# A Fourier filter ahead of a gated FFN: the transform in steps of four columns instead of two

## The chip, the cores and the metric

The kernel runs on one core of one Trainium2 chip. The metric is the device time of one execution in microseconds, the median of several runs. The engines are TensorE (PE in the profile, its weight loads PEld), VectorE (DVE), ScalarE (ACT), GpSimd (POOL) and SyncE (SP), which here only issues DMA transfers; a core has 16 DMA engines.

## What is computed

A filter is applied to a sequence of 3136 rows in the frequency domain, for 8 batches and 256 channels, and the result goes through an FFN with a gate that is a convolution over three rows.

```python
def _attn_ref(x, filt_r, filt_i):          # x: 8 x 3136 x 256
    X = np.fft.rfft(x, axis=1)
    Y = X * (filt_r + 1j * filt_i)[None]
    return np.fft.irfft(Y, n=x.shape[1], axis=1).astype(np.float32)

def _moe_ref(x, w_in, conv_w, w_out):      # 256 -> 1024 -> 256, kernel of 3
    h = np.maximum(x @ w_in, 0.0)
    conv_out = ...                         # sum over k of conv_w[k] * h shifted by k - 1
    gate = 1.0 / (1.0 + np.exp(-conv_out))
    return (h * gate @ w_out).astype(np.float32)
```

The weights of the FFN come as 64-bit numbers, which the kernel converts itself.

## The kernel before

The length is split as 3136 = 112 x 28, and the transform is four matrix products with steps through DRAM between them.

- **First** (L317 to L322): for one of the 28 columns, 112 rows of x by a 112 x 112 matrix in `s1_sb`. A step does two columns in one PSUM bank (`ps`); `store` (L307) copies them to `sa` on ACT and sends them to `a_dram`.
- **Second** (L324 to L332): for two of the 28 frequency groups `a` is loaded from `a_dram` and multiplied by `s2_sb` (for the last group `s2s_sb`) into `pp`. It needs all 28 columns of its batch in `a_dram`.
- **The filter** (`filt`, L334 to L345): three products on DVE read `pp`: L340 writes `u`, by the real parts in `t1_sb`; L341 and L342 write the two halves of `v`, by the imaginary parts in `t2_sb`. Real and imaginary rows lie on partitions 0 to 55 and 64 to 119, and L341 and L342 cross over. POOL adds `u` and `v` to `z` (L344). `u` has two buffers (the pool's default), `z` three, and `v` is one of two fixed tiles in turn.
- **Third** (L347 to L352): `z` by `i1_sb`, copied to `sb` on ACT and sent to `b_dram`.
- **Last** (`last_load`, `last_stage`, `last_out`): two columns are loaded from `b_dram` into `br`, multiplied by `m2_sb`, and split into a high part (`hi_act` on ACT) and a low part (`lo_dve` on DVE, L149) of `y`, which the FFN reads. Batch 0 is done at the end of the transform, the other batches between the FFN's steps.

The loop at L369 runs over steps `i` of two columns or groups, 14 to a batch. Step `i` does the first transform of step `i - 1`, and with `m = i - 18` the second of `m - 1`, the filter of `m - 2` and the third of `m - 4`. Four engines keep the order in which the code is written; SP's transfers stand in an order close to it. On TensorE a step is third, first, second. x is loaded seven steps ahead (8 buffers), a three steps ahead (5). At the beginning the tables arrive piece by piece: parts of the filter (`load_filter`, L246) go to partitions 0 to 63 of `t1_sb` and `t2_sb`, and ACT copies them to partitions 64 to 119, the imaginary ones with a factor of -1 (L251 to L254). From step 22 on, `convert_weights` makes fp32 of the weights in short DVE instructions (L160 to L172), a POOL sum (L174) and copies, at most one piece in a step. From step 118 on the last transform of batch 0 goes along with the rest, two columns in a step.

Behind the loop the FFN runs over pieces of 448 rows and 128 of its 1024 inner channels (L502 to L522); each product there is three matmuls of high and low parts. PSUM's eight banks are five for `ps` and three for `pp` in the transform, and are given to the FFN's pools after it.

## Time and profile before

| | |
|---|---|
| median of 3 runs | 1573.16 us (1568.74 to 1574.19) |
| the profiled execution | 1572.45 us |
| its span, first to last instruction | 1570.7 us |
| TensorE busy | 1505.0 us (96%), 9424 matmul instructions |
| DVE, ACT, POOL busy | 1280.6, 1189.3, 697.4 us |
| moved by DMA | 166.83 MB |

Times in the profile count from the span's start. A group of instructions is named by its line, engine, operation and tiles (out<-in); its idle time is that of the engine just before such instructions, with the releasers that ended most of it. A matmul of fp32 stands there as two instructions, so "x4" is the two matmuls of a step. Ends of matmuls are modelled, so that starts of matmuls are the better clock.

### The profile page before, as it was taken

The page shows a single profiled execution, that of the slowest core. Times are in us where ns is not written, and L with a number is a line of the kernel's source. Part 1 is how long each engine was busy: PE and PEld are TensorE (multiplying, and loading weights), DVE is VectorE, ACT ScalarE, POOL GpSimd, SP SyncE. Part 2 cuts the span into 40 slices and gives each one's busy share as a digit, 9 for nine tenths or more (in the row PEclk, how much of TensorE's full clock was granted, in tenths as well). Part 3 has the DMA queues.
Part 4 walks back from the last instruction along what each step waited for, and adds up shares of the span by engine and source line. Part 5 has one row for each costly group of instructions (what it writes and reads, how often), then busy time and mean ns, then how long its engine had stood idle before and what let it go on. Part 6 is the DMA issues. An engine that isn't in the chain of part 4 may idle for free.

```text
span 1570.7 us, 26429 instructions
## 1 busy us (share of the span) xinstructions
PE 1505.0 (96%) x9424; PEld 1346.7 (86%) x9424; DVE 1280.6 (82%) x1965; ACT 1189.3 (76%) x2162; POOL 697.4 (44%) x624
## 2 busy tenths in 40 slices
PE   5699999988999999999999999999999999999998
PEld 3356666656999999999999999999999999999998
DVE  0478888888888888888888888888888888888887
ACT  3444444435888888888888888888888888888887
POOL 0255555553444444444444444444444434444444
PEclk9799999999999999999999999999999999999999
DMA  9999999984111011111101111111111111100001
GB/s 285 288 321 337 342 342 346 328 283 140 30 48 48 30 48 48 48 48 48 47 25 36 48 53 48 47 45 47 36 42 48 48 43 36 48 25 24 24 25 48
DMA packets 128278, 166.83 MB, mean 106 GB/s; under 512 B 10682, under 2 KB 87571, under 8 KB 128147
## 3 DMA queue, kind: packets, MB, share of 16 engines
q1 hardware_dynamic: 128147, 165.14, 33.0%
q8 instruction: 75, 1.23, 0.3%
q14 instruction: 56, 0.46, 0.1%
HBM read 88.03 MB, written 77.07 MB: 105 GB/s over the span
## 4 chain that ended last, share of the span: by engine, by line
PE 83%; DMA 10%; DVE 3%; issue 1%; ACT 1%; SPq 1%; POOL 1%; ACTq 0%; DVEq 0%; POOLq 0%
PE ps_h L178 12%; PE ps_h L179 12%; PE ps_h L177 11%; PE po L473 11%; PE po L475 11%; PE po L474 11%; PE ps_h L216 6%; DMA a<-a_dram 4%; PE pp L328 3%; PE ps L351 3%; PE ps L321 2%; DMA a_dram<-sa 2%; DMA t_sb<-in_fi 1%; DVE y L149 1%; DVE v L341 1%
## 5 line engine op out<-in xcount | busy, mean ns | idle before, releaser
L152 POOL TENSOR_TENSOR g<-t,g 128x448 fp32r<-128x448 f32 x448 | 517.2, 1154 | 666.9 <-ACT g L146 262.8
L473 PE MATMUL po<-wo,g 128*128 128x256 f32 x1568 | 441.6, 282 | 0.0
L475 PE MATMUL po<-wo,g 128*128 128x256 f32 x1568 | 433.9, 277 | 0.0
L474 PE MATMUL po<-wo,g 128*128 128x256 f32 x1568 | 433.6, 277 | 0.0
L447 DVE SCALAR_TENSOR_TENSOR t<-ps_h,cw,t 128x448 f32<-128x448 f32 x448 | 305.5, 682 | 83.2 <-ACT t L442 72.9
L178 PE MATMUL ps_h<-y,wi 128*128 128x450 f32 x896 | 330.4, 369 | 4.5 <-DVE y L149 4.5
L177 PE MATMUL ps_h<-y,wi 128*128 128x450 f32 x896 | 328.8, 367 | 3.0 <-ACT y L146 1.6
L179 PE MATMUL ps_h<-y,wi 128*128 128x450 f32 x896 | 328.8, 367 | 0.0
L448 DVE SCALAR_TENSOR_TENSOR t<-ps_h,cw,t 128x448 f32<-128x448 f32 x448 | 306.4, 684 | 16.0
L442 ACT ACTIVATE t<-ps_h,cw 128x448 f32<-128x448 f32 x448 | 284.8, 636 | 42.6 <-ACT ps_h L440 1.9
L473 PEld LDWEIGHTS po<-wo,g 128*128 128x128 f32 x1568 | 294.8, 188 | 7.0
L474 PEld LDWEIGHTS po<-wo,g 128*128 128x128 f32 x1568 | 294.4, 188 | 5.7
L475 PEld LDWEIGHTS po<-wo,g 128*128 128x128 f32 x1568 | 294.5, 188 | 0.0
L440 ACT ACTIVATE ps_h<-ps_h 128x450 f32<-128x450 f32 x448 | 252.0, 562 | 31.6 <-PE ps_h L179 26.8
L453 DVE TENSOR_TENSOR t<-ps_h,t 128x448 f32<-128x448 f32 x448 | 275.1, 614 | 0.1
L452 ACT ACTIVATE t<-t 128x448 f32<-128x448 f32 x448 | 255.0, 569 | 12.2 <-DVE t L448 11.2
L146 ACT ACTIVATE g<-t 128x448 fp32r<-128x448 f32 x448 | 254.6, 568 | 0.2 <-DVE t L453 0.2
L344 POOL TENSOR_TENSOR z<-u,v 120x512 f32<-120x512 f32 x112 | 157.0, 1402 | 181.4 <-DVE v L342 164.8
L309 ACT ACTIVATE sb<-ps 112x512 f32<-112x512 f32 x112 | 66.9, 597 | 161.5 <-DMA b_dram<-sb 86.7
L179 PEld LDWEIGHTS ps_h<-y,wi 128*128 128x128 f32 x896 | 168.3, 188 | 13.9
L177 PEld LDWEIGHTS ps_h<-y,wi 128*128 128x128 f32 x896 | 170.1, 190 | 11.6 <-ACT y L146 2.8
L178 PEld LDWEIGHTS ps_h<-y,wi 128*128 128x128 f32 x896 | 168.3, 188 | 13.5 <-DVE y L149 6.7
(51 smaller groups left out, 1475.0 us busy)
## 6 DMA issues: line engine op xcount, KB each, us to landing
x<-in_x SPq DMA_DIRECT2D x112, 224.0 KB, 4.9
a_dram<-sa SPq DMA_DIRECT2D x112, 224.0 KB, 4.6
a<-a_dram SPq DMA_DIRECT2D x112, 224.0 KB, 4.6
b_dram<-sb SPq DMA_DIRECT2D x112, 224.0 KB, 4.4
br<-b_dram SPq DMA_DIRECT2D x112, 224.0 KB, 2.6
out<-ot SPq DMA_DIRECT2D x27, 896.0 KB, 4.1
raw<-in_w_in SPq DMA_DIRECT2D x8, 256.0 KB, 5.2
raw<-in_w_out SPq DMA_DIRECT2D x8, 256.0 KB, 6.1
```

Source lines behind the costliest of these rows:

```text
L152: nc.gpsimd.tensor_tensor(out=dst, in0=src, in1=hi.bitcast(F32), op=ALU.subtract)
L177: nc.tensor.matmul(ps, lhsT=wh, rhs=rh, start=start, stop=False, **kw)
L178: nc.tensor.matmul(ps, lhsT=wh, rhs=rl, start=False, stop=False, **kw)
L179: nc.tensor.matmul(ps, lhsT=wl, rhs=rh, start=False, stop=stop, **kw)
L442: nc.scalar.activation(t, h[:, 1:SUB + 1], AF.Copy, scale=cw[:, 1, f:f + 1])
L447: nc.vector.scalar_tensor_tensor(out=t, in0=h[:, 0:SUB], scalar=cw[:, 0, f:f + 1], in1=t, op0=ALU.mult, op1=ALU.add)
L448: nc.vector.scalar_tensor_tensor(out=t, in0=h[:, 2:SUB + 2], scalar=cw[:, 2, f:f + 1], in1=t, op0=ALU.mult, op1=ALU.add)
L452: nc.scalar.activation(t, t, AF.Sigmoid)
L453: nc.vector.tensor_mul(t, h[:, 1:SUB + 1], t)
L473: nc.tensor.matmul(o, lhsT=gh[:, sl], rhs=wo[0][:, f], start=first, stop=False, skip_group_check=True)
L474: nc.tensor.matmul(o, lhsT=gh[:, sl], rhs=wo[1][:, f], start=False, stop=False, skip_group_check=True)
L475: nc.tensor.matmul(o, lhsT=gl[:, sl], rhs=wo[0][:, f], start=False, stop=last, skip_group_check=True)
```

## The change

A step does four columns or four groups, and there are 7 steps to a batch instead of 14. Loads and stores of x, sa, a and sb are twice as large and half as many. PSUM tiles of the transform take two banks, two for first and third (`bank_pair`) and two for `pp`, eight banks as before. The buffers are x 4, a 3, sa and sb 2, z 2 and u 1, each of double size. In a step TensorE's order is first, third, second; the third transform is that of `m - 2`, with `m = i - 9`. Loads of a stand one step ahead. Table pieces come at steps 4 to 10. The imaginary parts of the filter are loaded to partitions 56 to 119 and copied down to 0 to 55 without a sign; L349 of the new kernel multiplies by -1 as well. Conversion of the weights takes up to two pieces in a step, from step 11 on, with one buffer for `ws` instead of two. The last transform of batch 0 takes four columns in a step. The FFN's code is the same.

```diff
-        return np.concatenate([re, gap, im, -im, gap, re], 1)
+        return np.concatenate([re, gap, im], 1)
...
-    def last_load(b, c):
-        br = lp.tile([112, 2, D], F32, name="br", bufs=4)
-        nc.sync.dma_start(out=br, in_=b_dram[b][c:c + 2].rearrange("n p d -> p n d"))
+    def last_load(b, c, n=2):
+        br = lp.tile([112, n, D], F32, name=f"br{n}", bufs=4 if n == 2 else 2)
+        nc.sync.dma_start(out=br, in_=b_dram[b][c:c + n].rearrange("n p d -> p n d"))
         lasts[b, c] = br
...
-    def last_stage(b, c, ps):
+    def last_stage(b, c, ps, n=2):

         br = lasts[b, c]
-        for j in range(2):
+        if n == 2:
+            pv = ps[:, 0:4 * N1].rearrange("p (k c a) -> p k c a", c=2, a=N1)
+        else:
+            pv = ps.rearrange("p (k e) -> p k e", k=KT)[:, :, 0:n * N1].rearrange("p k (c a) -> p k c a", a=N1)
+        for j in range(n):
             for k in range(KT):
-                o = ps[:, (2 * k + j) * N1:(2 * k + j + 1) * N1]
-                nc.tensor.matmul(o, lhsT=br[:, j, 128 * k:128 * k + 128], rhs=m2_sb, start=True, stop=True)
-        lasts[b, c] = ps
-
-    def last_out(b, c):
-        yh, yl = y_slices(b, slice(c, c + 2))
-        pv = lasts.pop((b, c))[:, 0:4 * N1].rearrange("p (k c a) -> p k c a", c=2, a=N1)
+                nc.tensor.matmul(pv[:, k, j], lhsT=br[:, j, 128 * k:128 * k + 128], rhs=m2_sb, start=True, stop=True)
+        lasts[b, c] = pv
+
+    def last_out(b, c, n=2):
+        yh, yl = y_slices(b, slice(c, c + n))
+        pv = lasts.pop((b, c))
         hi_act(yh, pv)
         lo_dve(yl, pv, yh)
...
+    NQ = 7
+    SKEW = 9
...
         tc.tile_pool(name="fp", bufs=2) as fp,
-        tc.tile_pool(name="cv", bufs=2) as cv,
-        tc.tile_pool(name="fps", bufs=5, space=bass.MemoryType.PSUM) as fps,
+        tc.tile_pool(name="fps", bufs=2, space=bass.MemoryType.PSUM) as fps,
     ):
...
-        turned = [fc.tile([120, 2, D], F32, name=f"v{k}") for k in range(2)]
+        turned = [fc.tile([120, 4, D], F32, name=f"v{k}") for k in range(2)]
...
-        def load_filter(c):
+        parts = {}
+        psums = {}
+        raws = {}
+
+        def load_tables(c):
+
             sl = slice(4 * c, 4 * c + 4)
-            for t, src in ((t1_sb, fr), (t2_sb, fi)):
-                nc.sync.dma_start(out=t[0:64, sl], in_=src[:, sl])
+            nc.sync.dma_start(out=t1_sb[0:64, sl], in_=fr[:, sl])
+            nc.sync.dma_start(out=t2_sb[56:120, sl], in_=fi[:, sl])
+            nc.sync.dma_start(out=i1_sb[:, sl], in_=i1[:, sl])

         def copy_filter(c):
             sl = slice(4 * c, 4 * c + 4)
             nc.scalar.activation(t1_sb[64:120, sl], t1_sb[0:56, sl], AF.Copy)
-            nc.scalar.activation(t2_sb[64:120, sl], t2_sb[0:56, sl], AF.Copy, scale=-1.0)
+            nc.scalar.activation(t2_sb[0:56, sl], t2_sb[64:120, sl], AF.Copy)
...
-                ws = cv.tile([128, 2, 256], F32, name="ws")
+                ws = cv.tile([128, 2, 256], F32, name="ws", bufs=1)
...
-                    yield
+                yield
...
+        def load(kind, b, q):
             if kind == "x":
+                r = xp.tile([112, 4, D], F32, name="x", bufs=4)
...
+                r = fp.tile([112, 4, D], F32, name="a", bufs=3)
...
+
+        def store(kind, b, q, ps):
+            st = (xp if kind == "sa" else fp).tile([112, 4, D], F32, name=kind, bufs=2)
...
+        def bank_pair():
+            return fps.tile([128, 1024], F32, name="ps")
+
+        def first(b, q):
+            r = rows.pop(("x", b, q))
+            ps = bank_pair()[0:112].rearrange("p (n d) -> p n d", d=D)
+            for j in range(4):
+                nc.tensor.matmul(ps[:, j], lhsT=s1_sb[:, 4 * q + j], rhs=r[:, j], start=True, stop=True)
             return ps
...
-        def filt(b, p):
-
-
-            pp, v = psums.pop((b, p)), turned[p % 2]
-            sl = slice(2 * p, 2 * p + 2)
-            u = fp.tile([120, 2, D], F32, name="u")
+        def second(b, q):
+            r = rows.pop(("a", b, q))
+            pp = fps.tile([120, 4, D], F32, name="pp")
+            for j in (0, 2):
+                if j == 0 or q < NQ - 1:
+                    nc.tensor.matmul(pp[:, j:j + 2], lhsT=s2_sb, rhs=r[:, j:j + 2], start=True, stop=True)
+                else:
+                    nc.tensor.matmul(pp[:, 2], lhsT=s2_sb, rhs=r[:, 2], start=True, stop=True)
+                    nc.tensor.matmul(pp[:, 3], lhsT=s2s_sb, rhs=r[:, 3], start=True, stop=True)
+            psums[b, q] = pp
+
+        def filt(b, q):
+
+
+            pp, v = psums.pop((b, q)), turned[q % 2]
+            sl = slice(4 * q, 4 * q + 4)
+            u = fp.tile([120, 4, D], F32, name="u", bufs=1)
             nc.vector.tensor_mul(u, pp, t1_sb[:, sl])
             nc.vector.tensor_mul(v[64:120], pp[0:56], t2_sb[0:56, sl])
-            nc.vector.tensor_mul(v[0:56], pp[64:120], t2_sb[64:120, sl])
-            z = fp.tile([120, 2, D], F32, name="z", bufs=3)
+            nc.vector.scalar_tensor_tensor(out=v[0:56], in0=pp[64:120], scalar=-1.0, in1=t2_sb[64:120, sl], op0=ALU.mult, op1=ALU.mult)
+            z = fp.tile([120, 4, D], F32, name="z")
             nc.gpsimd.tensor_tensor(out=z, in0=u, in1=v, op=ALU.add)
-            parts["z", b, p] = z
-
-        def third(b, p):
-            z = parts.pop(("z", b, p))
-            ps = fps.tile([112, 2, D], F32, name="ps")
-            for j in range(2):
-                nc.tensor.matmul(ps[:, j], lhsT=i1_sb[:, 2 * p + j], rhs=z[:, j], start=True, stop=True)
+            parts[b, q] = z
...
-        SKEW = NP + 4
...
-        done = NP * B + 6
-        NI = max(NP * B + SKEW + 5, done + N2 // 2 + 3)
+        done = NQ * B + 2
+        NI = NQ * B + SKEW + 5
         with tc.manual_schedule(engines=COMPUTE):
...
                 if i == done:
+                    for _ in wsteps:
+                        pass
...
-                if 1 <= i < 4:
-                    nc.sync.dma_start(out=s1_sb[:, 4 * i + 12:4 * i + 16], in_=s1[:, 4 * i + 12:4 * i + 16])
-                if (bp := at(f + 7)) and i:
+                if i < 3:
+                    nc.sync.dma_start(out=s1_sb[:, 4 * i + 16:4 * i + 20], in_=s1[:, 4 * i + 16:4 * i + 20])
+                if (bp := at(i + 3)) and i:
                     load("x", *bp)
-                if bp := at(m + 3):
+                if bp := at(m + 1):
                     load("a", *bp)
-                if i == 6:
-                    nc.sync.dma_start(out=s2_sb, in_=s2[:, 0:120])
-                    nc.sync.dma_start(out=s2s_sb, in_=s2s[:, 0:120])
+                if i == 3:
+                    nc.sync.dma_start(out=s2_sb, in_=s2)
+                    nc.sync.dma_start(out=s2s_sb, in_=s2s)
                     nc.sync.dma_start(out=m2_sb, in_=m2)
-                if 12 <= i < 26 and i % 2 == 0:
-                    sl = slice((i - 12) // 2 * 4, (i - 12) // 2 * 4 + 4)
-                    load_filter(i // 2 - 6)
-                    nc.sync.dma_start(out=i1_sb[:, sl], in_=i1[:, sl])
-                if bp := at(m - 2):
+                if 4 <= i < 11:
+                    load_tables(i - 4)
+                if bp := at(m - 1):
                     filt(*bp)
-                pt = third(*bp) if (bp := at(m - 4)) else None
-                pf = first(*bp) if (bp := at(f - 1)) else None
-                if bp := at(m - 1):
+                pf = first(*bp) if (bp := at(i)) else None
+                if pf is not None:
+                    store("sa", *at(i), pf)
+                pt = third(*bp) if (bp := at(m - 2)) else None
+                if pt is not None:
+                    store("sb", *at(m - 2), pt)
+                if bp := at(m):
                     second(*bp)
-                if pt is not None:
-                    store("sb", *at(m - 4), pt)
-                if pf is not None:
-                    store("sa", *at(f - 1), pf)
-                if 3 <= i < 16:
-                    next(csteps, None)
-                if i == 16:
+                for _ in range(2):
+                    if 1 <= i < 8:
+                        next(csteps, None)
+                    if i >= 11:
+                        next(wsteps, None)
+                if i == 8:
                     load_weights(0)
                     load_weights(1)
-                if i >= 22 and i % 9 != 8:
-                    next(wsteps, None)
-                if 16 <= i < 30 and i % 2 == 0:
-                    copy_filter(i // 2 - 8)
-                c = 2 * (i - done)
+                if 7 <= i < 14:
+                    copy_filter(i - 7)
+                c = 4 * (i - done - 2)
+                if 0 <= c - 8 < N2:
+                    last_out(0, c - 8, 4)
                 if 0 <= c - 4 < N2:
-                    last_out(0, c - 4)
-                if 0 <= c - 2 < N2:
-                    last_stage(0, c - 2, fps.tile([128, 512], F32, name="ps"))
+                    last_stage(0, c - 4, bank_pair(), 4)
                 if 0 <= c < N2:
-                    last_load(0, c)
+                    last_load(0, c, 4)
...
+    fi = np.roll(fi, 8, 0)
```

On DVE, the first filter steps: `pp` is the second transform in PSUM, `t_sb` a part of the filter, `raw` and `em` are the weights' conversion; in brackets the semaphores that an instruction waits for (Pool is POOL's, PE TensorE's, DMAHW a transfer's). Before:

```order
L340 TENSOR_TENSOR u<-pp,t_sb 120x512 [waits DMAHW2_49,PE_49,Activation_49]
L341 TENSOR_TENSOR v_103<-pp,t_sb 56x512 [waits DMAHW3_49]
L342 TENSOR_TENSOR v_103<-pp,t_sb 56x512 [waits Activation_49,Pool_49]
L340 TENSOR_TENSOR u<-pp,t_sb 120x512 [waits PE_49]
L341 TENSOR_TENSOR v_104<-pp,t_sb 56x512
L342 TENSOR_TENSOR v_104<-pp,t_sb 56x512 [waits Pool_49]
L340 TENSOR_TENSOR u<-pp,t_sb 120x512 [waits PE_49,DMAHW1_49,Activation_49,Pool_49]
```

And after the change, at the same place:

```order
L347 TENSOR_TENSOR u<-pp,t_sb 120x1024 [waits DMAHW7_49,PE_49,Activation_49]
L348 TENSOR_TENSOR v_103<-pp,t_sb 56x1024 [waits Activation_49]
L349 SCALAR_TENSOR_TENSOR v_103<-pp,t_sb 56x1024 [waits DMAHW0_49,Pool_49]
L347 TENSOR_TENSOR u<-pp,t_sb 120x1024 [waits PE_49,DMAHW4_49,Activation_49,Pool_49]
L348 TENSOR_TENSOR v_104<-pp,t_sb 56x1024 [waits Activation_49]
L349 SCALAR_TENSOR_TENSOR v_104<-pp,t_sb 56x1024 [waits DMAHW5_49]
L160 TENSOR_SCALAR em<-raw 128x512 [waits DMAHW1_49,DMAHW0_49]
L162 TENSOR_SCALAR em<-raw 128x512
L347 TENSOR_TENSOR u<-pp,t_sb 120x1024 [waits PE_49,Activation_49,Pool_49]
```

The product into `u` waits for POOL from the third step on before and from the second on after, and two conversions stand together behind L349.

On SP, the transfers around the first load of a (`a_dram_57` is batch 0's, `a_dram_58` batch 1's; `in_fr`, `in_fi` and `in_i` are a piece of the tables). Before:

```order
L304 DMA x<-in_x 112x512
L249 DMA t_sb<-in_fr 64x1024
L249 DMA t_sb<-in_fi 64x1024
L388 DMA i_sb<-in_i 120x448
L315 DMA a_dram_57<-sa 112x2x256
L304 DMA x<-in_x 112x512
L315 DMA a_dram_58<-sa 112x2x256
L304 DMA x<-in_x 112x512
L304 DMA a<-a_dram_57 112x512 x2
```

And after:

```order
L318 DMA a_dram_57<-sa 112x4x256
L307 DMA x<-in_x 112x1024
L258 DMA t_sb<-in_fr 64x1024
L259 DMA t_sb<-in_fi 64x1024
L260 DMA i_sb<-in_i 120x448
L318 DMA a_dram_58<-sa 112x4x256
L307 DMA x<-in_x 112x1024
L307 DMA a<-a_dram_57 112x1024
L258 DMA t_sb<-in_fr 64x1024
```

Another piece of the tables has moved in between the last store of batch 0 and the first load that reads it; four of the seven pieces now stand ahead of that load, two before.

On DVE, the end of the transform (`y` and `ps` are the last transform of batch 0, L447 and L450 the first instructions of the FFN). Before:

```order
L149 TENSOR_TENSOR y_2840<-ps,y_2839 128x2x2x112
L340 TENSOR_TENSOR u<-pp,t_sb 120x512
L341 TENSOR_TENSOR v_104<-pp,t_sb 56x512
L342 TENSOR_TENSOR v_104<-pp,t_sb 56x512
L149 TENSOR_TENSOR y_2840<-ps,y_2839 128x2x2x112 x3
L447 SCALAR_TENSOR_TENSOR t<-ps_h,cw,t 128x448
```

And after:

```order
L149 TENSOR_TENSOR y_1899<-ps,y_1898 128x2x4x112
L347 TENSOR_TENSOR u<-pp,t_sb 120x1024
L348 TENSOR_TENSOR v_103<-pp,t_sb 56x1024
L349 SCALAR_TENSOR_TENSOR v_103<-pp,t_sb 56x1024
L149 TENSOR_TENSOR y_1899<-ps,y_1898 128x2x4x112 x4
L450 SCALAR_TENSOR_TENSOR t<-ps_h,cw,t 128x448
```

Of the subtractions for `y` now four of four columns stand behind the last filter step, where three of two columns stood.

More of the change, by code (lines that the diff above doesn't have):

```diff
@@ L230, in tile_fft_filter_gated_ffn @@
         tc.tile_pool(name="fp", bufs=2) as fp,
-        tc.tile_pool(name="cv", bufs=2) as cv,
-        tc.tile_pool(name="fps", bufs=5, space=bass.MemoryType.PSUM) as fps,
+        tc.tile_pool(name="fps", bufs=2, space=bass.MemoryType.PSUM) as fps,
     ):
+        cv = forward_pools.enter_context(tc.tile_pool(name="cv", bufs=2))
         s2_sb = fc.tile([112, 120], F32, name="s2_sb")
@@ L315, in store @@
             nc.sync.dma_start(out=v, in_=st)
-        def first(b, p):
-            r = rows.pop(("x", b, p))
-            ps = fps.tile([112, 2, D], F32, name="ps")
-            for j in range(2):
-                nc.tensor.matmul(ps[:, j], lhsT=s1_sb[:, 2 * p + j], rhs=r[:, j], start=True, stop=True)
-            return ps
-        def second(b, p):
-            r = rows.pop(("a", b, p))
-            pp = fps.tile([120, 2, D], F32, name="pp", bufs=3)
-            if p < NP - 1:
-                nc.tensor.matmul(pp, lhsT=s2_sb, rhs=r, start=True, stop=True)
-            else:
-                for j, m in ((0, s2_sb), (1, s2s_sb)):
-                    nc.tensor.matmul(pp[:, j], lhsT=m, rhs=r[:, j], start=True, stop=True)
-            psums[b, p] = pp
@@ L344, in filt, with third @@
             nc.gpsimd.tensor_tensor(out=z, in0=u, in1=v, op=ALU.add)
-            parts["z", b, p] = z
-        def third(b, p):
-            z = parts.pop(("z", b, p))
-            ps = fps.tile([112, 2, D], F32, name="ps")
-            for j in range(2):
-                nc.tensor.matmul(ps[:, j], lhsT=i1_sb[:, 2 * p + j], rhs=z[:, j], start=True, stop=True)
+            parts[b, q] = z
+        def third(b, q):
+            z = parts.pop((b, q))
+            ps = bank_pair()[0:112].rearrange("p (n d) -> p n d", d=D)
+            for j in range(4):
+                nc.tensor.matmul(ps[:, j], lhsT=i1_sb[:, 4 * q + j], rhs=z[:, j], start=True, stop=True)
@@ L352, in third @@
             return ps
         def at(i):
-            return divmod(i, NP) if 0 <= i < NP * B else None
-        SKEW = NP + 4
-        nc.sync.dma_start(out=s1_sb[:, 0:4], in_=s1[:, 0:4])
-        load("x", 0, 0)
-        load("x", 0, 1)
-        for c in range(1, 4):
+            return divmod(i, NQ) if 0 <= i < NQ * B else None
+        for c in range(4):
             nc.sync.dma_start(out=s1_sb[:, 4 * c:4 * c + 4], in_=s1[:, 4 * c:4 * c + 4])
-            load("x", 0, 2 * c)
-            load("x", 0, 2 * c + 1)
+            load("x", 0, c)
```

18 lines of the change are left out of this document (4 added, 14 removed).

## The prediction

> **What bounds the kernel now.** I read the slices of the page first: the DMA engines are full for some 340 us and nearly idle after. Then the engines by stretch, cut where that changes: one row for each (start:end, length, busy us and instructions of PE, PEld, DVE, ACT, POOL, then granted clock, DMA share, GB/s):
>
> ```profile
> 0.00:46.00 46.00, 25.15 (x79) 15.85 (x80) 1.18 (x8) 16.83 (x25) 1.51 (x8) 0.86 0.97 283
> 46.00:91.00 45.00, 33.90 (x101) 20.23 (x100) 26.52 (x40) 21.21 (x30) 15.72 (x11) 0.84 1.04 302
> 91.00:321.00 230.00, 216.08 (x831) 145.20 (x830) 192.16 (x289) 100.82 (x178) 131.95 (x103) 1.00 1.00 336
> ...
> 384.00:1571.00 1187.00, 1177.37 (x8175) 1129.56 (x8173) 1004.55 (x1552) 1023.71 (x1892) 518.13 (x476) 1.00 0.13 41
> ```
>
> The last stretch, the gated FFN, is 1187 us of full TensorE, and its code is not touched. So the question is only when it begins. The transform before it has a filling part, a steady part (91 to 321) and a tail. TensorE in the steady part, in order of time (start, length, what):
>
> ```profile
> 92.32 1.03 PE L321 MATMUL ps<-x,s_sb 112*112 112x256 f32 x4
> ...
> 94.91 1.03 PE L321 MATMUL ps<-x,s_sb 112*112 112x256 f32 x4
> ...
> 320.53 1.03 PE L321 MATMUL ps<-x,s_sb 112*112 112x256 f32 x4
> ```
>
> From one first transform to the next is 2.59 us when nothing is waited for (94.91 - 92.32), a third of it, 0.86, for each of the three transforms. From 92.32 to 320.53 there are 81 steps: 2.82 us each, 5.63 for two. TensorE at 2.59 and a DMA share of 1.00 are almost in balance. The waits of that stretch (in all, times, longest):
>
> ```profile
> PE pp L328 <- DMA a<-a_dram: 12.1, 14, 1.9
> ...
> DVE u L340 <- POOL z L344: 1.1, 1, 1.1
> ```
>
> TensorE waits for loads of a. DVE almost never waits for POOL (once): `u` has two buffers, so the products of one step run while POOL still adds those of the last.
>
> **The change, part by part. The loop through u.** `u` is doubled in size and has one buffer. L347 writes it first, L348 and L349 follow on DVE, and POOL's sum (L351 of the new kernel) reads it; so the next L347 waits until the sum of the step before has ended. DVE's three products and POOL's sum, which ran beside each other, now run one after the other. The prices, groups by line and shape (busy, mean ns of one, idle before):
>
> ```profile
> L344 POOL TENSOR_TENSOR z<-u,v 120x512 f32<-120x512 f32 x112 | 157.0, 1402 | 181.4 <-DVE v L342 164.8 <-PE pp L328 10.6 <-PE ps L351 4.7
> L342 DVE TENSOR_TENSOR v<-pp,t_sb 56x512 f32<-56x512 f32 x112 | 77.6, 693 | 3.3
> L340 DVE TENSOR_TENSOR u<-pp,t_sb 120x512 f32<-120x512 f32 x112 | 77.3, 690 | 75.7 <-PE pp L328 67.0 <-POOL z L344 2.3 <-ACT t_sb L254 2.3
> L341 DVE TENSOR_TENSOR v<-pp,t_sb 56x512 f32<-56x512 f32 x112 | 76.6, 684 | 2.9
> L149 DVE TENSOR_TENSOR y<-ps,y 128x448 fp32r<-128x448 f32 x13 | 13.1, 1010 | 2.9 <-ACT y L146 2.4
> L174 POOL TENSOR_TENSOR ws<-ws,em 128x512 f32<-128x512 f32 x8 | 10.2, 1269 | 0.0
> L253 ACT ACTIVATE t_sb<-t_sb 56x1024 f32<-56x1024 f32 x7 | 7.4, 1055 | 0.2
> L164 DVE TENSOR_TENSOR em<-em 128x512 int32<-128x512 int32 x8 | 5.5, 693 | 0.2
> L168 DVE SCALAR_TENSOR_TENSOR ws<-em 128x512 f32<-128x512 int32 x8 | 5.5, 693 | 0.2
> L174 POOL TENSOR_TENSOR cw<-cw,em 128x24 f32<-128x24 f32 x1 | 0.2, 233 | 18.5 <-DVE em L172 18.5
> L164 DVE TENSOR_TENSOR em<-em 128x24 int32<-128x24 int32 x1 | 0.2, 184 | 0.0
> ```
>
> L164 at 512 and at 24 elements gives DVE (693 - 184)/488 = 1.043 ns an element, so 512 more cost 0.534 us and the products become 1.224, 1.218 and 1.227: 3.67 us. L174 gives POOL (1269 - 233)/488 = 2.12 ns, so 512 more cost 1.09 us. What stands between them, and what holds a sum back, in order of time:
>
> ```profile
> 319.90 0.69 DVE L164 TENSOR_TENSOR em<-em 128x512 int32<-128x512 int32 x1
> 320.63 0.69 DVE L340 TENSOR_TENSOR u<-pp,t_sb 120x512 f32<-120x512 f32 x1
> 322.75 0.43 DVE L166 TENSOR_SCALAR em<-raw 128x512 int32<-128x512 int32 x1
> ...
> 332.92 0.69 DVE L342 TENSOR_TENSOR v<-pp,t_sb 56x512 f32<-56x512 f32 x1
> ```
>
> ```profile
> 320.04 1.69 POOL L344 TENSOR_TENSOR z<-u,v 120x512 f32<-120x512 f32 x1 [1.20 <-DVE v L342]
> 322.89 1.42 POOL L344 TENSOR_TENSOR z<-u,v 120x512 f32<-120x512 f32 x1 [1.17 <-DVE v L342]
> ...
> 333.78 1.27 POOL L344 TENSOR_TENSOR z<-u,v 120x512 f32<-120x512 f32 x1 [1.17 <-PE ps L351]
> ```
>
> ```profile
> 60.11 1.50 POOL L344 TENSOR_TENSOR z<-u,v 120x512 f32<-120x512 f32 x1 [7.32 <-DVE v L342]
> ...
> 61.71 0.69 DVE L340 TENSOR_TENSOR u<-pp,t_sb 120x512 f32<-120x512 f32 x1 [1.21 <-POOL z L344]
> ```
>
> Undisturbed, the sum takes 1.27, so 2.36 at the new size. From L342's end (333.61) to the sum's start are 0.17, from a sum's end (61.61) to the next L340 are 0.10, between two DVE instructions some 0.035. The loop: 3.67 + 0.07 + 0.17 + 2.36 + 0.10 = **6.37 us** a step, where two old steps took 5.63.
>
> **Conversions beside the sum.** Where DVE converts weights right behind L342, the sum ends later: 321.73 is 1.14 behind L164's end (320.59), 324.31 is 1.13 behind L166's end (323.18), while an undisturbed one ends 1.44 behind L342. So 0.69 us of conversion delays it by 0.41 and 0.43 us by 0.15. The new kernel puts up to two conversions there: 0.43 + 0.43, twice 0.69 + 0.43, one 0.69, none, in a cycle of five steps. If both hold the sum back, that is 0.61 + 0.87 + 0.87 + 0.41 + 0 = 2.76, or 0.55 a step; if the first alone, 0.15 + 3 x 0.41 = 1.38, or 0.28. I take 0.55: a second conversion that yields to the sum would run behind it, and `u` behind that. It falls on steps 11 to 50.
>
> **Filling.** Tables come earlier: four of the seven pieces now stand ahead of the first load of a, two before. The sizes (KB of each issue, us to landing):
>
> ```profile
> x<-in_x SPq DMA_DIRECT2D x112, 224.0 KB, 4.9
> ...
> t_sb<-in_fr SPq DMA_DIRECT2D x7, 256.0 KB, 6.3
> ...
> i_sb<-in_i SPq DMA_DIRECT2D x7, 210.0 KB, 6.5
> ```
>
> Through the fourth load of a the program issues 30 transfers of 448 KB (15 x, 11 sa, 4 a), 7 table pieces of 256 + 256 + 210 KB, 1 MB of weights and 1.5 MB of s1 and small tables: 21.6 MB. At the old pace (283 GB/s for 46 us, 302 after) they are in at 74.4. With the second transform (1.73) and its handoff the product of group 3 starts at 76.5. Until there the DMA queues set the pace, behind it the loop. Filter parts in different halves and rows of 4 KB could make it 5 us earlier, a queue blocked on SP 4 later.
>
> **Tail.** The last sum and the second FFN matmul of before:
>
> ```profile
> 378.54 1.28 POOL L344 TENSOR_TENSOR z<-u,v 120x512 f32<-120x512 f32 x1 [1.76 <-DVE v L342]
> ...
> 383.61 0.47 PE L178 MATMUL ps_h<-y,wi 128*128 128x450 f32 x1 [0.54 <-DVE y L149]
> ```
>
> The FFN gets going at 383.61, 3.8 behind the last sum's end (379.82). L149 takes 1.01 for two columns, 1.9 for four (2.02 doubled, 1.86 with 0.16 of it fixed). Behind the last sum now stand the third transform (1.73 and 0.3 of handoffs), the copy to sb (1.06, as L253 at that size), three hi copies and one subtraction at 1.9: 10.7. Three subtractions stand between two filters, behind a hi copy that waits for the sb copy; each makes its step some 0.5 longer: 1.5.
>
> **Sum.** 76.5 + 53 loops x 6.37 (337.6) + 38 x 0.55 (20.9) + 1.5 + 10.7 = 447.2 against 383.6: +63.6. The profiled execution took 1572.45 (span 1570.7), 0.7 less than the median of the three runs, so the forecast is **1636 us**.
>
> **At nothing.** DMA: four transfers of 448 KB a step at 336 GB/s are 5.46 us, under 6.37; DMA stops being the bound, and a load issued one step ahead has more than a step to land. TensorE: 5.18 of 6.37. PSUM: a pair of banks is copied in 1.06 while TensorE does the two other transforms, 3.45. If the loop were gone, these would be the bound again. The factor -1 moves from ACT to L349: L168 costs what L164 does (693), so nothing; with a source in PSUM the form costs 0.07 more elsewhere (L447 and L453 of the FFN, same size), at most 4 us for 56 steps:
>
> ```profile
> L447 DVE SCALAR_TENSOR_TENSOR t<-ps_h,cw,t 128x448 f32<-128x448 f32 x448 | 305.5, 682 | 83.2 <-ACT t L442 72.9
> ...
> L453 DVE TENSOR_TENSOR t<-ps_h,t 128x448 f32<-128x448 f32 x448 | 275.1, 614 | 0.1
> ```
>
> **Rivals.** *TensorE sets the pace, faster (0.06).* If POOL's sum of 1024 came out under 1.6 us, the loop would be under 5.63 and no longer bind; the transfers with half the packets would then let TensorE run at 2.59 a half step: 81 x 0.23 = 18.6 gained, and 5 in the tail, where for each of 10 filters three fixed parts of 0.16 go: **1549**. For it: the DMA share of 1.00 and TensorE's waits for a. Against it: a sum of 512 takes 1.27 at best here, and L174 shows the price growing with the elements. [...]
>
> *No change (0.02):* loop and gain cancel, if the conversions cost nothing and the filling gains its most, and the loop is 5.6.
>
> *TensorE falls to half clock in the loop's gaps, much slower (0.02).* Rows of before:
>
> ```profile
> 86.25 1.09 PE L328 MATMUL pp<-a,s_sb 112*120 112x512 f32 x2 [1.74 <-DMA a<-a_dram]
> 88.53 1.91 PE L321 MATMUL ps<-x,s_sb 112*112 112x256 f32 x4
> ...
> 187.03 1.09 PE L328 MATMUL pp<-a,s_sb 112*120 112x512 f32 x2 [1.86 <-DMA a<-a_dram]
> 188.82 1.03 PE L321 MATMUL ps<-x,s_sb 112*112 112x256 f32 x4
> ```
>
> After a wait of 1.74 the next matmuls were slow (1.91 for 1.03), after one of 1.86 they were not. The loop leaves gaps of 1.2 to 2. At half clock a step is 10.36 of TensorE: 52 x (10.36 - 6.92) = 179 more, **1815**. Against it: at half clock TensorE would be busy all the time, and it has 2.9 us of room between a third transform's start and the time its second is needed. [...]
>
> **How the numbers follow.** The loop has 0.90. Its own bounds: conversions 0.28 (-10), filling -5, tail -2 at the low end (1619); L349 +4, filling +4, a sum grown from the mean of 1.40 instead of 1.27 (+7), tail +2 at the high end (1653). The range, 1612 to 1655, goes a little past both ends and leaves out the rivals. Differences under 0.5% (8 us) are about what a measurement of this kernel cannot tell from none. Faster 0.06, same 0.02, slower 0.92.
>
> **What would show it.** In the new profile `DVE u` waits for `POOL z` in nearly every step, about 2.5 us each; u starts 6.4 to 7.2 us apart; DMA share is 0.8 to 0.9 in the steady part; the FFN begins near 447. The prediction is wrong if u waits for TensorE or a load instead, if z takes under 2 us, or if the FFN stretch itself is longer than 1187.

## The result, and the profile after

The changed kernel takes **1637.66 us** (median of 4 runs, 1637.01 to 1639.96), beside 1572.70 us of the kernel before in the same comparison: ratio 1.042 with a 95% interval of 1.0398 to 1.0441. The forecast was 1636 us, the range 1612 to 1655. The page and the windows of the new profile (columns as in the prediction):

```profile
span 1635.6 us, 25256 instructions
...
0.00:46.00 46.00, 25.86 (x80) 17.30 (x80) 1.17 (x7) 14.82 (x15) 2.37 (x8) 0.81 1.00 281
46.00:91.00 45.00, 28.55 (x88) 17.24 (x89) 24.45 (x19) 19.76 (x20) 10.47 (x4) 0.78 1.03 296
91.00:321.00 230.00, 187.08 (x700) 121.81 (x699) 191.24 (x152) 75.16 (x84) 107.30 (x55) 1.00 0.96 291
321.00:384.00 63.00, 49.95 (x179) 31.90 (x178) 39.96 (x34) 17.44 (x19) 26.85 (x13) 0.97 0.78 234
384.00:447.00 63.00, 45.39 (x206) 31.63 (x204) 37.86 (x29) 21.01 (x16) 19.02 (x12) 0.92 0.57 162
447.00:1635.00 1188.00, 1177.52 (x8176) 1129.71 (x8175) 1006.37 (x1553) 1023.76 (x1892) 518.19 (x476) 1.00 0.13 41
```

The FFN's stretch is what it was: from its second product to the end of the span 1187.2 us (1635.6 - 448.39) against 1187.1 (1570.7 - 383.61). All of the loss lies ahead of it: in 91 to 321 TensorE does 700 matmul instructions where it did 831. The groups of the transform (0 to 450):

```profile
L351 POOL TENSOR_TENSOR z<-u,v 120x1024 f32<-120x1024 f32 x56 | 142.7, 2548 | 249.7 <-DVE v L349 187.5 <-PE pp L335 49.3 <-PE pp L338 9.1
...
L349 DVE SCALAR_TENSOR_TENSOR v<-pp,t_sb 56x1024 f32<-56x1024 f32 x56 | 68.7, 1226 | 1.0
L347 DVE TENSOR_TENSOR u<-pp,t_sb 120x1024 f32<-120x1024 f32 x56 | 68.6, 1225 | 116.1 <-POOL z L351 65.9 <-PE pp L335 49.5
L348 DVE TENSOR_TENSOR v<-pp,t_sb 56x1024 f32<-56x1024 f32 x56 | 68.2, 1218 | 1.0
L166 DVE TENSOR_SCALAR em<-raw 128x512 int32<-128x512 int32 x8 | 19.6, 2454 | 0.3
L170 DVE TENSOR_SCALAR em<-ws 128x512 int32<-128x512 int32 x8 | 19.6, 2453 | 0.3
L162 DVE TENSOR_SCALAR em<-raw 128x512 int32<-128x512 int32 x8 | 18.4, 2305 | 0.0
...
L160 DVE TENSOR_SCALAR em<-raw 128x512 int32<-128x512 int32 x8 | 3.4, 427 | 0.3
```

The products came out as worked out. The wait of `u` for POOL is 65.9 us in all, less than the prediction's 2.5 us for nearly each of 53 steps. The rest hides in busy time: L162, L166 and L170 take 2.3 to 2.45 us, though L160, the same operation on the same shape, takes 0.43. DVE and then POOL, in order of time:

```profile
136.93 1.22 DVE L347 TENSOR_TENSOR u<-pp,t_sb 120x1024 f32<-120x1024 f32 x1 [2.54 <-POOL z L351]
...
143.60 1.23 DVE L347 TENSOR_TENSOR u<-pp,t_sb 120x1024 f32<-120x1024 f32 x1
...
147.33 0.69 DVE L164 TENSOR_TENSOR em<-em 128x512 int32<-128x512 int32 x1
148.06 2.45 DVE L166 TENSOR_SCALAR em<-raw 128x512 int32<-128x512 int32 x1
150.54 1.23 DVE L347 TENSOR_TENSOR u<-pp,t_sb 120x1024 f32<-120x1024 f32 x1
...
157.48 1.22 DVE L347 TENSOR_TENSOR u<-pp,t_sb 120x1024 f32<-120x1024 f32 x1
...
164.13 1.23 DVE L347 TENSOR_TENSOR u<-pp,t_sb 120x1024 f32<-120x1024 f32 x1 [2.23 <-POOL z L351]
...
166.60 1.23 DVE L349 SCALAR_TENSOR_TENSOR v<-pp,t_sb 56x1024 f32<-56x1024 f32 x1
170.38 1.23 DVE L347 TENSOR_TENSOR u<-pp,t_sb 120x1024 f32<-120x1024 f32 x1 [2.55 <-POOL z L351]
```

```profile
147.47 2.75 POOL L351 TENSOR_TENSOR z<-u,v 120x1024 f32<-120x1024 f32 x1 [4.18 <-DVE v L349]
...
168.00 2.35 POOL L351 TENSOR_TENSOR z<-u,v 120x1024 f32<-120x1024 f32 x1 [2.67 <-PE pp L335]
```

Without conversions `u` starts 6.25 us apart (170.38 - 164.13). With L164 and L166 the sum starts during L164 and is 0.4 longer; L166 starts during the sum and ends at 150.51, 0.29 behind the sum's end (150.22). A conversion that begins beside the sum costs 0.43 and waits some 2, and `u` stands behind it.

### The profile page after: what moved, and what is told of

Same layout as the page of the kernel before. It is cut to its first block, busy times and chain, and to the rows that moved or that the text cites. A ratio compares the mean times of both kernels' runs of the same rounds, so it can differ in the third digit from the quotient of the medians.

```text
span 1635.6 us, 25256 instructions
## 1 busy us (share of the span) xinstructions
PE 1514.3 (93%) x9424; PEld 1349.6 (83%) x9424; DVE 1301.1 (80%) x1790; ACT 1171.9 (72%) x2043; POOL 684.2 (42%) x568
## 4 chain that ended last, share of the span: by engine, by line
PE 71%; DVE 1%; ACT 1%; issue 0%
PE ps_h L178 11%; PE ps_h L179 11%; PE ps_h L177 11%; PE po L476 11%; PE po L478 11%; PE po L477 11%; PE ps_h L219 5%; ACT y L146 1%; DVE y L149 1%; DVE t L451 0%; PE ps L219 0%; DVE t L450 0%; DVE t L456 0%; ACT sb L312 0%; ACT t L445 0%
## 5 line engine op out<-in xcount | busy, mean ns | idle before, releaser
L450 DVE SCALAR_TENSOR_TENSOR t<-ps_h,cw,t 128x448 f32<-128x448 f32 x448 | 305.9, 683 | 82.1 <-ACT t L445 71.4
L351 POOL TENSOR_TENSOR z<-u,v 120x1024 f32<-120x1024 f32 x56 | 142.7, 2548 | 249.7 <-DVE v L349 187.5
L358 PE MATMUL ps<-z,i_sb 120*112 120x256 f32 x448 | 115.2, 402 | 68.1 <-POOL z L351 62.5
```

The costliest lines, as they stand in the source:

```text
L450: nc.vector.scalar_tensor_tensor(out=t, in0=h[:, 0:SUB], scalar=cw[:, 0, f:f + 1], in1=t, op0=ALU.mult, op1=ALU.add)
```

## The experiments

Each ran beside the kernel before on the same chip; over these comparisons the kernel before had medians of 1571.18 to 1572.70 us. The edit is against the changed kernel unless another is named.

| run | median us | ratio, 95% interval |
|---|---|---|
| changed kernel | 1637.66 | 1.042 (1.0398 to 1.0441) |
| u_two | 1612.94 | 1.0262 (1.0228 to 1.0297) |
| u_last | 1603.68 | 1.0204 (1.0174 to 1.0233) |
| u_last_mid | 1588.21 | 1.0104 (1.0076 to 1.0132) |
| old_u_one | 1658.80 | 1.0554 (1.0519 to 1.0589) |
| one_half | 1642.99 | 1.0453 (1.0434 to 1.0473) |
| split_loads | 1588.77 | 1.0104 (1.0088 to 1.0121) |
| tables_later | 1589.25 | 1.0110 (1.0091 to 1.0129) |
| tail_early | 1589.43 | 1.0111 (1.0088 to 1.0133) |
| late_third | 1576.51 | 1.0030 (1.0011 to 1.0048) |
| late_third_tail | 1573.45 | 1.0012 (0.9996 to 1.0029) |
| out_first | 1564.44 | 0.9955 (0.9942 to 0.9968) |
| out_first_tables | 1561.76 | 0.9939 (0.9924 to 0.9954) |

**The single buffer put into the kernel before.**

```diff
-            u = fp.tile([120, 2, D], F32, name="u")
+            u = fp.tile([120, 2, D], F32, name="u", bufs=1)
```

> The kernel before with one buffer for u and nothing else changed. Theory: the loop binds there too: 0.69 + 0.68 + 0.69 + 0.07 + 0.14 + 1.27 + 0.03 = 3.57 us a step of two, and some 0.13 for conversions, where 2.82 were: from about 75 us on 105 steps of 3.7: 1655 us (1638 to 1670). Rival, that one buffer is harmless and the step's size costs the time: 1573.

Its waits (91 to 321):

```profile
DVE u L340 <- POOL z L344: 79.9, 62, 1.5
```

The wait that was 1.1 us in all is 79.9, and the loss is larger than that of the whole change: the loop through one `u` is enough by itself. In the steps without conversions `u` starts 3.56 us apart there, 7.12 for four columns where the changed kernel takes 6.25: by the means before and after, three products of 512 elements twice are 4.13 us and three of 1024 are 3.67, two sums of 1.27 are 2.54 and one of the double size is 2.35, and the gaps between them come half as often at four.

**Two buffers for u in the changed kernel** (the four-column `br` gives up one of its two to make room).

```diff
-            u = fp.tile([120, 4, D], F32, name="u", bufs=1)
+            u = fp.tile([120, 4, D], F32, name="u")
-        br = lp.tile([112, n, D], F32, name=f"br{n}", bufs=4 if n == 2 else 2)
+        br = lp.tile([112, n, D], F32, name=f"br{n}", bufs=4 if n == 2 else 1)
```

> The changed kernel with two buffers for u; the room comes from the four-column tile of the last transform (br), which has one buffer instead of two. Theory: the loop through u is gone, so steps without conversions fall from 6.25 us to what TensorE (5.18) or DMA (5.4 to 6.0) allows. In steps with two conversions the second one runs behind POOL's sum (2.45 us where it takes 0.43), and the next product stands behind it, so 24 steps stay at 6.7 to 6.9. 29 steps gain 0.3 to 1 us: 1612 us (1600 to 1622). If the second conversion did not matter: about 1580. Rival, that steps of four columns as such (larger rows in DMA, fewer buffers, PSUM pairs) set the pace and u's buffer is beside the point: 1630 or more.

25 us of 65 come back. On DVE the conversions still hold `u` up, now without any wait for its buffer:

```profile
145.72 2.45 DVE L166 TENSOR_SCALAR em<-raw 128x512 int32<-128x512 int32 x1
148.20 1.23 DVE L347 TENSOR_TENSOR u<-pp,t_sb 120x1024 f32<-120x1024 f32 x1
...
152.65 2.45 DVE L170 TENSOR_SCALAR em<-ws 128x512 int32<-128x512 int32 x1
155.13 1.23 DVE L347 TENSOR_TENSOR u<-pp,t_sb 120x1024 f32<-120x1024 f32 x1
```

The step is 6.93 us (155.13 - 148.20), as with one buffer: there were two loops of nearly one length, and to cut one shows the other. The 25 us are what is left after the price of the room: with one buffer of `br`, 17.32 us lie between the last sum's end and the FFN's second product (403.69 to 421.01), where the changed kernel has 14.83; in `u_two` the last piece waits 3.94 us there for its load.

**u as the last of the three products** (still one buffer), so that only it waits for the sum.

```diff
-            nc.vector.tensor_mul(u, pp, t1_sb[:, sl])
             nc.vector.tensor_mul(v[64:120], pp[0:56], t2_sb[0:56, sl])
             nc.vector.scalar_tensor_tensor(out=v[0:56], in0=pp[64:120], scalar=-1.0, ...)
+            nc.vector.tensor_mul(u, pp, t1_sb[:, sl])
```

> The changed kernel, same buffers, with the product into u as the last of the three on DVE instead of the first. Theory: u is then held only for its own product and the sum (1.22 + 0.14 + 2.34 + 0.03 = 3.7 us a step), so it no longer binds; the second conversion behind the sum still does. Within 6 us of the run with two buffers: 1610 us (1600 to 1622). Rival, that the step's size sets the pace: 1630 or more.

34 us come back, 9 more than with two buffers, where at most 6 were expected between the two. Of the 4.6 us between their profiled executions (1610.88 and 1606.26), 2.6 lie behind the last sum (17.32 and 14.71 us), where `u_two` has the single `br`. The conversions still begin beside the sum: L166 takes 2.46 us in this run too.

**The same, with the conversions between the second product and u**, where POOL is still idle.

```diff
             nc.vector.scalar_tensor_tensor(out=v[0:56], in0=pp[64:120], scalar=-1.0, ...)
+            for _ in range(2):
+                if i >= 11:
+                    next(wsteps, None)
             nc.vector.tensor_mul(u, pp, t1_sb[:, sl])
...
-                    if i >= 11:
-                        next(wsteps, None)
```

> As the run before, and the two conversions of a step stand on DVE between the second product and the product into u, so that none is beside POOL's sum. Theory: DVE has at most 3.7 + 1.2 = 4.9 us a step and no wait for POOL; TensorE (5.18) or DMA sets the pace, 53 steps at 5.2 to 6.0 instead of 6.6: 1586 us (1560 to 1605), no conversion over 0.7 us. If the conversions behind the sum cost nothing: as the run before. Rival, step size: 1630 or more.

One of its groups on DVE, its window, and TensorE's wait for the sum (91 to 340):

```profile
L166 DVE TENSOR_SCALAR em<-raw 128x512 int32<-128x512 int32 x8 | 3.4, 427 | 0.3
...
91.00:321.00 230.00, 218.18 (x826) 145.67 (x825) 174.67 (x172) 88.36 (x98) 116.56 (x65) 0.99 1.03 335
...
PE ps L361 <- POOL z L354: 15.5, 21, 2.0
```

The conversions are 0.43 again (L162 and L170 too), and the order of DVE alone brought 49 us of 65 back without a byte of memory. The 16 us left are the subject of the runs below.

**The filter's imaginary parts in the lower half again**, copied upward by ACT with the factor of -1, and L349 plain, as before.

```diff
-            nc.sync.dma_start(out=t2_sb[56:120, sl], in_=fi[:, sl])
+            nc.sync.dma_start(out=t2_sb[0:64, sl], in_=fi[:, sl])
...
```

> The changed kernel with the imaginary filter parts loaded to partitions 0 to 63 as before, copied up with the factor -1, and L349 a plain product again: that part of the change alone undone. Theory: both forms of L349 take 1.23 us and ACT has room, so only the filling could feel it: 1638 us (1633 to 1644), no change that can be told. Rival, that two halves relieve the transfers to 64 partitions: 4 to 7 us slower, 1643.

It is 5 us slower, at the edge of what the two intervals tell apart; but the trace puts the loss in one place. The product of group 3 starts at 88.21, not 83.48, the FFN's second product at 452.24, not 448.39:

```profile
88.21 1.23 DVE L347 TENSOR_TENSOR u<-pp,t_sb 120x1024 f32<-120x1024 f32 x1
```

```profile
452.24 0.74 PE L178 MATMUL ps_h<-y,wi 128*128 128x450 f32 x1 [1.13 <-DVE y L149]
```

By these two profiles the placement of the filter parts is worth 4 to 5 us in the filling. One profile of each is thin evidence: TensorE's second transform of group 3 starts at 85.85 in this run, and between 80.27 and 83.92 in the nine others that have the parts in two halves and the pieces at the same steps, so 2 to 5.6 us earlier. Why the placement helps stays open.

**Three edits of u_last_mid that changed nothing,** though each was expected to gain. Transfers of x and a in two pieces with rows of 2 KB:

```diff
-            nc.sync.dma_start(out=r, in_=v[:, 4 * q:4 * q + 4])
+            for h in (0, 2):
+                nc.sync.dma_start(out=r[:, h:h + 2], in_=v[:, 4 * q + h:4 * q + h + 2])
```

> As the run with u last and the conversions in the middle (1588 us), with every load of x and a as two transfers of two columns (rows of 2 KB instead of 4 KB) into the same tile. Theory: the DMA engines are what is left as the bound there (share 1.03 at 335 GB/s), and a row of 4 KB is no cheaper than two of 2 KB but dearer (200 ns in the mean against 2 x 95 in the kernel before); with rows of 2 KB the steps fall to 5.3: 1573 us (1564 to 1582). Rival, that larger rows help: 1590 to 1600. Rival, TensorE or waits are the bound: 1588.

Table pieces two steps later, their copies one:

```diff
-                if 4 <= i < 11:
-                    load_tables(i - 4)
+                if 6 <= i < 13:
+                    load_tables(i - 6)
-                if 7 <= i < 14:
-                    copy_filter(i - 7)
+                if 8 <= i < 15:
+                    copy_filter(i - 8)
```

> As the run with u last and the conversions in the middle, with the seven table pieces two steps later (steps 6 to 12, copies at 8 to 14), so that two of them stand ahead of the first load of a, as in the kernel before. Theory: the first second transform comes 4 to 6 us sooner, part of it is given back when the later pieces come: 1584 us (1579 to 1588). Rival, the order in the filling is beside the point since the bytes are the same: 1588.

The last transform of batch 0 two steps earlier:

```diff
-                c = 4 * (i - done - 2)
+                c = 4 * (i - done)
```

> As the run with u last and the conversions in the middle, with the last transform of batch 0 begun two steps sooner. Theory: in the steps with it the third transform waits for DVE's subtraction to free one of two PSUM pairs (6.8 us a step instead of some 5); two more steps pay that (+3.6), and two pieces less stand behind the last sum (-7): 1585 us (1580 to 1588). Rival, the end is set by the filter steps alone: 1581.

All three lie within 1.3 us of u_last_mid. The pattern of long and short steps was the same with split transfers and with later tables (in 91 to 321 TensorE does 823 and 820 instructions at 335 and 336 GB/s, where u_last_mid does 826 at 335), so neither packets nor tables set it; with later tables the product of group 3 came 4 us earlier, which was gone some steps later (TensorE does 92 instructions in 46 to 91 where u_last_mid does 86, and both have done 992 by 321). With the earlier end the last sum ended later by what was saved behind it (the third transform behind it starts at 393.27 for 387.47, the FFN's second product at 399.94 for 399.84). What was left was a chain of engines: the third transform stands on TensorE ahead of the second of its step and waits for a sum of the same step.

**The third transform a step later** (u_last_mid with a third `z`, `br` as in u_two).

```diff
-            z = fp.tile([120, 4, D], F32, name="z")
+            z = fp.tile([120, 4, D], F32, name="z", bufs=3)
-                pt = third(*bp) if (bp := at(m - 2)) else None
+                pt = third(*bp) if (bp := at(m - 3)) else None
...
-                    store("sb", *at(m - 2), pt)
+                    store("sb", *at(m - 3), pt)
```

> u_last_mid with the third transform one step later (of m - 3 instead of m - 2), z with three buffers, and one buffer for the four-column br. Theory 1, TensorE's third transform waits for POOL's sum of the same step, and the chain second, filter, sum, third, second over two steps sets 5.6 us a step: with a step between sum and third the steps come down to what the transfers take, 4 x 448 KB at 335 GB/s = 5.46, at best TensorE's 5.2; 53 steps gain 8 to 20, some of it lost again because the last third stands a step further back: about 1579 (1570 to 1584). In its trace the idle time of TensorE's third before POOL's z is gone. Theory 2, the transfers set 5.6 whatever the engines do: 1588, and TensorE waits for loads of a instead.

Its wait for the sum (91 to 340) and its window:

```profile
PE ps L361 <- POOL z L354: 0.5, 1, 0.5
...
91.00:321.00 230.00, 222.08 (x860) 151.55 (x858) 183.27 (x179) 91.99 (x101) 121.60 (x67) 1.00 1.03 347
```

15.0 us of waiting are gone, and TensorE does 860 instructions in the stretch, more than the 831 of the kernel before. What keeps it at 1.003 is the end, the last sum and the FFN's second product:

```profile
365.23 2.38 POOL L354 TENSOR_TENSOR z<-u,v 120x1024 f32<-120x1024 f32 x1 [4.56 <-DVE u L352]
...
384.44 0.58 PE L178 MATMUL ps_h<-y,wi 128*128 128x450 f32 x1
```

The last sum ends at 367.61, 12.2 us earlier than before, but from there to the FFN it is 16.8 us, where before had 3.8.

**The end.** late_third with the last transform of batch 0 two steps earlier (the edit of tail_early):

> late_third with the last transform of batch 0 starting two steps earlier. Theory 1, what stands behind the last sum (three of the seven pieces of batch 0's last transform) is exposed: two pieces fewer behind it, each some 2 to 2.5 us, and each makes a filter step longer by at most 1: about 4 less than late_third. Theory 2, the pieces cost in the loop what they save behind it, as they did with the third one step earlier: the same as late_third.

The steps with `y` still took 6.8 us, and the two ratios are not told apart. Then, on top of it, a finished piece's copies ahead of the step's others, and two buffers for each `br`:

```diff
                     filt(*bp, i)
+                c = 4 * (i - done)
+                if 0 <= c - 8 < N2:
+                    last_out(0, c - 8, 4)
...
-                c = 4 * (i - done)
-                if 0 <= c - 8 < N2:
-                    last_out(0, c - 8, 4)
...
-bufs=4 if n == 2 else 1
+bufs=2
```

> late_third_tail with the copies of a finished piece of batch 0's last transform (hi on ACT, subtraction on DVE) ahead of the step's other copies instead of behind them, and two buffers for the four-column br again (two for the two-column one). Theory 1, the steps of 6.8 us at the end are a chain third, copy to sb, hi, subtraction, next piece, next third, all in one step because the next piece waits for the pair of banks that the subtraction reads: with hi and subtraction first, only DVE's 3.7 + 1.8 = 5.5 us are left a step, so that five such steps gain some 6 and the stretch behind the last sum falls under 8: about 1566 (1562 to 1570), under the kernel before by some 0.3 per cent. Theory 2, the load of br (one buffer, landing after 6 us) set 6.8 alone or the gain is taken by something behind it: 1570 to 1574.

And with the tables of tables_later as well:

> out_first with the table pieces two steps and their copies one step later, as in the earlier run. Theory 1, the filling ends 4 us earlier and now that the steps have room the later pieces hold nothing up: 4 less than out_first. Theory 2, steps 4 to 8 wait for the later pieces again and give it back: the same as out_first.

DVE at the end of out_first_tables, the sum that runs beside these rows, and the FFN's second product:

```profile
358.61 1.23 DVE L352 TENSOR_TENSOR u<-pp,t_sb 120x1024 f32<-120x1024 f32 x1
359.75 1.83 DVE L149 TENSOR_TENSOR y<-ps,y 128x896 fp32r<-128x896 f32 x1
361.61 1.22 DVE L347 TENSOR_TENSOR v<-pp,t_sb 56x1024 f32<-56x1024 f32 x1
...
364.10 1.22 DVE L352 TENSOR_TENSOR u<-pp,t_sb 120x1024 f32<-120x1024 f32 x1
```

```profile
359.97 2.38 POOL L354 TENSOR_TENSOR z<-u,v 120x1024 f32<-120x1024 f32 x1 [3.14 <-PE pp L338]
```

```profile
374.17 0.37 PE L178 MATMUL ps_h<-y,wi 128*128 128x450 f32 x1
```

The steps at the end are 5.49 us (364.10 - 358.61), DVE without a gap, and the FFN begins at 374.17, 9.4 ahead of the kernel before. The kernel with steps of four columns is 0.6% faster (0.5 to 0.8 by the interval), once `u`, the conversions, the third transform and the copies of `y` stand where little waits for them. How much of that is due to the four columns isn't shown: the same orders weren't tried with two. Whether the order of the copies or the second `br` buffer freed the last steps wasn't tried apart, and the later tables (2.7 us between the medians) lie within the two intervals.

## Why the prediction was right, step by step

- **The loop through u** is what made the change slower: old_u_one makes it alone, u_two and u_last take it away. Its size was 6.25 us, not 6.37: from the first product's start to the third's end 3.70 where 3.74 were taken (164.13 to 167.83), and from the sum's end to `u` 0.03 where 0.10 were (170.35 to 170.38). 53 x 0.12 = 6.4 us too much. All told `u` starts 6.24 to 6.99 us apart, where 6.4 to 7.2 were forecast.
- **Conversions beside the sum** were forecast with the right mechanism ("a second conversion that yields to the sum would run behind it, and `u` behind that") and 0.55 us a step. The figure itself was worked out for another case, in which both conversions hold the sum back; in the trace the first makes the sum 0.17 or 0.40 longer and the second ends 0.29 behind it. That the size came out near is partly luck. The five kinds of step measure 6.67, 6.94, 6.94, 6.65 and 6.25 (from one `u` to the next in the DVE rows above), so 0.42, 0.69, 0.69, 0.40 and 0 over 6.25: 0.44 on average, 4.2 us too much in 38 steps.
- **Filling** was sized too short. The product of group 3 was put at 76.5 and starts at 83.48. TensorE's second transforms of groups 1 and 3, and DVE's products of groups 1 to 3:

```profile
66.03 3.54 PE L335 MATMUL pp<-a,s_sb 112*120 112x512 f32 x4 [6.28 <-DMA a<-a_dram]
...
81.15 1.95 PE L335 MATMUL pp<-a,s_sb 112*120 112x512 f32 x4 [1.39 <-DMA a<-a_dram]
```

```profile
69.78 1.23 DVE L347 TENSOR_TENSOR u<-pp,t_sb 120x1024 f32<-120x1024 f32 x1 [8.97 <-PE pp L335]
...
76.50 1.23 DVE L347 TENSOR_TENSOR u<-pp,t_sb 120x1024 f32<-120x1024 f32 x1
...
83.48 1.23 DVE L347 TENSOR_TENSOR u<-pp,t_sb 120x1024 f32<-120x1024 f32 x1
```

  From group 1 on DVE has no idle time ahead of `u`: the steps are 6.72 and 6.98 us, and the prediction let the loop begin two groups later. But the load was late on its own. In `u_last_mid`, where neither `u` nor a conversion holds the products up, the second transform of group 3 starts at the same time, and the first product only 0.3 earlier than here:

```profile
81.12 1.95 PE L335 MATMUL pp<-a,s_sb 112*120 112x512 f32 x4 [2.09 <-DMA a<-a_dram]
```

```profile
83.18 1.22 DVE L347 TENSOR_TENSOR v<-pp,t_sb 56x1024 f32<-56x1024 f32 x1 [2.58 <-PE pp L335]
```

  So the count of bytes is what failed, with 81.15 for 74.4. It took in the transfers issued up to that load, 21.6 MB, and 302 GB/s from 46 us on. The windows of the trace give some 22.9 MB by 81.15 (46 us at 281 GB/s and 35.15 at 285, an estimate). Six more transfers were issued between the load (70.21) and its use; that they took their share of the engines while the load was under way fits the difference, but wasn't tried. The 5 us that the prediction left for filter parts in different halves and rows of 4 KB were the author's estimate, with no number of a run beside it: for the halves one_half shows 4.7 (88.21 - 83.48), and with rows of 2 KB the time was the same (split_loads, 1588.77 for 1588.21).
- **Tail:** 10.7 forecast, 14.83 measured (433.56 to 448.39). In order of time:

```profile
431.18 2.38 POOL L351 TENSOR_TENSOR z<-u,v 120x1024 f32<-120x1024 f32 x1 [4.40 <-DVE v L349]
...
434.33 3.63 PE L358 MATMUL ps<-z,i_sb 120*112 120x256 f32 x8 [1.62 <-DVE y L149]
...
441.20 1.80 ACT L146 ACTIVATE y<-ps 128x896 fp32r<-128x896 f32 x1 [0.41 <-PE ps L219]
442.65 1.86 PEld L219 LDWEIGHTS ps<-m_sb,br 112*128 112x128 f32 x16 [1.67 <-DVE y L149]
...
444.73 1.79 ACT L146 ACTIVATE y<-ps 128x896 fp32r<-128x896 f32 x1 [1.73 <-PE ps L219]
...
448.39 0.74 PE L178 MATMUL ps_h<-y,wi 128*128 128x450 f32 x1 [1.36 <-DVE y L149]
```

  The terms themselves were right or small (1.8 for 1.9). What was left out are three waits: the third transform starts 0.77 behind the sum, because a subtraction that ends at 434.18 still holds its banks, and runs at half clock, 3.63 for 1.95 (granted clock 0.52); and two pieces of `y` share one pair of banks, so that a hi copy waits 1.73 for a product that waits for the subtraction. The prediction costed PSUM at nothing, with the cover of the two other transforms; at the end that cover is gone.
- **The sum:** +7.0 filling, -6.4 loop, -4.2 conversions, -0.1 steps with `y` (6.56, 6.84 and 6.77 us), +0.7 for one step near the end (6.92 us, 394.00 to 400.92, with transforms at a granted clock of 0.50 to 0.55), +4.1 tail: 1.1 over 447.2. That the forecast hit within 2 us was luck: four of its terms were off by 4 to 7 us each, and they cancelled. The mechanism, and the range, did not need that luck.
- **At nothing.** L349 with its factor takes 1226 ns beside L348's 1218: nothing, as said. That the transfers leave the bound held (291 GB/s for 336), but the DMA share stayed at 0.96 in 91 to 321, above the 0.8 to 0.9 forecast.
- **Rivals.** TensorE as the pace lost because the sum takes 2.35, not under 1.6. That half the packets make the transfers faster, as this rival took it, no run shows by itself: with loads of x and a in pieces of 224 or of 448 KB the time was the same (split_loads, 1588.77 for 1588.21). Half clock did not rule the steady part (granted clock 1.00 in 91 to 321); a lower clock came in the filling (0.81 and 0.78), as before (0.86 and 0.84), and in a few stretches near the end (0.69 in 393 to 404). In the kernels with the loops cut, the rival's direction did come: 347 GB/s in late_third, and 1561.76 us at best, where the rival put 1549.

## What to carry to other kernels

When tiles are doubled and buffers halved for room, look for every tile with one buffer that one engine writes first and another reads last: its two engines run in turn, and the step is the sum of both (here 3.70 us of DVE and 2.35 of POOL in 6.25). Write such a tile last, and put side work where the other engine is idle (L166 took 0.43 us there, 2.45 beside the sum), before asking for memory. Look for waits in the busy times too: L166 took 2.45 us where L160 took 0.43, and ended some 0.29 behind the sum each time.

## What the runs showed of the hardware

DVE's one-input conversions L166 and L170 (`TENSOR_SCALAR`, 128 x 512, 0.43 us) take 2.45 when they start during POOL's sum and end 0.29 behind it (150.51 and 150.22); a two-input one that starts first (L164) makes the sum 0.4 longer (2.75 for 2.35); a product that reads PSUM runs beside the sum at its usual 1.22 (in out_first_tables L347 at 361.61, with the sum from 359.97 to 362.35). What makes one wait for the other the trace does not show.

A DMA share near 1 did not mean full DMA engines. It was 1.00 at 336 GB/s before, 0.96 at 291 after the change, and 1.03 at 335 and at 347 in u_last_mid and late_third, so that the 1.00 which the prediction read as full engines left room. The GB/s and what TensorE waits for tell more.

A wait of 1.62 us stood ahead of a transform at half clock (434.33, 3.63 us, granted clock 0.52); at the same place in u_last_mid a wait of 1.60 did not bring it:

```profile
387.47 1.95 PE L361 MATMUL ps<-z,i_sb 120*112 120x256 f32 x8 [1.60 <-DVE y L149]
```

Nor does a longer wait decide by its length alone: in the changed kernel a third transform behind 2.56 us (387.74) took 1.98 us at a granted clock of 1.00, and the next, behind 2.57 (394.01), took 3.75 at 0.50. What fixes the moment stays open.
